# 128 tokens of a second expert ahead of the routing tail, one slot list, and out scatters that may overlap

## The chip, the cores and the metric

The kernel runs on one core of a Trainium2 chip. The core has five engines that work side by side: TensorE (PE) multiplies matrices, VectorE (DVE), ScalarE (ACT) and GpSimd (POOL) work on tiles, and SyncE (SP) issues most of the transfers. Each takes its instructions in the order in which they are queued. The metric is the device time of one execution in microseconds (us).

## The reference

An attention layer feeds a mixing layer with a two-matmul network (F = 2048), and that feeds a layer of eight experts. Only the last is touched by the change. Cut to what matters:

```python
B, S, D, E, F = (4, 576, 512, 8, 1024)
for b in range(B):
    prev_e = -1
    for s in range(S):
        fresh_e = argmax(logits[b, s])
        e = fresh_e if s == 0 or local_gate[b, s] < 0.5 else (prev_e if prev_e >= 0 else fresh_e)
        prev_e = e
        out[b, s] = p[e] * (relu(x[b, s] @ w1[e]) @ w2[e])
```

Every token goes to one expert. Which one depends on the tokens before it in its row of the batch, so an expert's last tokens are known only when the last rows of x are done.

## The kernel before

**Layout.** The 2304 tokens are 18 tiles of 128, taken in nine groups of two (the lists `GA` and `GB`). Matmuls take a number as a high and a low part (`split`: ScalarE casts the high part, VectorE subtracts for the low one), and `mm3` makes three matmuls of a product. `ffn` runs a two-matmul network in steps: for each of the eight 128-wide pieces f of the hidden layer 12 matmuls into `hps` (columns: the tokens), then ScalarE and VectorE make the hidden tile `h` (its ReLU and its low part) from it, and one step later 3 matmuls of 512 columns for each 128 tokens add into `acc`.

**The stages that the change touches.** While the mixing layer's second half runs over the groups 0 to 8, each finished group is routed: `finish_group` transposes its rows (`x2T`), `route` makes logits and one-hots, `assign` turns them into slot numbers, and GpSimd scatters an entry (row, token, gate) for each token into a list in HBM. An expert's slots are contiguous in it, in the order of its tokens. There are three lists (`slots0` to `slots2`), so that the last three scatters go to different ones; a reader loads all three and adds them.

After three of the four rows of the batch `first_expert` picks the expert with the most tokens so far, and `early` gathers its first 256 tokens (EARLY) and its weights: the early pass, an `ffn` over these, runs right behind group 8. Beside it, group 8 is routed and assigned, and `ranks` orders the experts: rank 0 is the early one, the others follow by size. Then one `ffn` runs for each rank, with room for CAPS[r] tokens (224 more of rank 0, 384 of rank 1, then 320, 320, 296, 272, 232, 216). What does not fit is done in a loop behind a branch, which these inputs do not take.

For each rank `expert_inputs` loads the slots, makes indices of them (`idn`), gathers the rows from `x2d` in HBM with an indirect transfer on GpSimd (`xg`), and transposes them (`tps`, then `xTe`). `expert_weights` loads 4 MB in four chunks of two 512 KB pieces into two raw tiles (`we`) and splits each piece in two. The split weights lie in two sets of four chunks (`wpA`, `wpB`), used in turn. `emit` scales the result by the gate (`yo`) and scatters it to `out`; each scatter waits for the one before, since both write `out`.

**What sets the order.** The code advances side work in generators (`beside`, `soon`, `pre_`) by some steps after each step of `ffn`. Each engine then has one fixed queue, in an order that the tool makes from this; `issue_after` keeps an instruction behind another.

Of the kernel before, what the change touches and what calls it, by code (L numbers as in the profile page):

```python
# [10 lines left out]
F32 = mybir.dt.float32  # L11
# [12 lines left out]
DM = H * D  # L24
# [14 lines left out]
EARLY = TM * P  # L39
CB = 256  # L40
# [32 lines left out]
CAPS = (224, 384, 320, 320, 296, 272, 232, 216)  # L73
# [20 lines left out]
LISTS = {GIDX[B - 1, 2]: 0, GIDX[B - 1, 3]: 1, GIDX[B - 2, 4]: 2}  # L94
NL = 3
# [16 lines left out]
def constants():  # L112
# [35 lines left out]
    c["rev"] = (float(E) - 1 - np.arange(E, dtype=np.float32))[None].copy()  # L148
    c["over"] = (P - 1 - np.array(CAPS, np.int32))[None].copy()
# [16 lines left out]
def build(ctx, tc, a, out):  # L166
# [5 lines left out]
    def split(hi, lo, src, eng=None):  # L172
        nc.scalar.copy(hi, src)  # L173
        return (eng or nc.vector).tensor_tensor(out=lo, in0=src, in1=hi.bitcast(F32), op=ALU.subtract)  # L174
# [33 lines left out]
    slots = [dram.tile([NSLOT, 4], F32, name=f"slots{i}") for i in range(NL)]  # L208
# [418 lines left out]
    def ffn(xT, n, chunks, ps_h, acc, hidden, sums, tail=0):  # L627
# [6 lines left out]
        for f in range(nf + 1):  # L634
# [16 lines left out]
            if f > 0:  # L651
# [3 lines left out]
                for t, c in enumerate(range(0, n, P)):  # L655
                    if g == 0:
                        acc.append(sums[t % len(sums)].tile([P, DM], F32, tag=("acc0", "acc1", "acc2", "g")[t], name="acc"))
# [5 lines left out]
                    mm3(acc[t][0:m], h[:, c:c + m], h[:, low + c:low + c + m], t2[:, 0, g % per], t2[:, 1, g % per], g == 0, g == nf - 1)  # L663
# [13 lines left out]
    rows_of, room = {}, []  # L677
# [125 lines left out]
    def setup():  # L803

        load = last["load"].ins
        with tc.issue_after(load):
            nc.sync.dma_start(out=ent, in_=a["ent"])
            for i in range(NL):
                nc.sync.dma_start(out=slots[i], in_=a["empty"][min(i, 1)])
# [309 lines left out]
    def assign(b, half=None):  # L1119
# [13 lines left out]
        for t in ts:  # L1133
# [12 lines left out]
            for j in range(2):  # L1146
# [15 lines left out]
    nc.sync.dma_start(out=over, in_=a["over"])  # L1162
    order = keep.tile([1, 2, E], F32, name="order")
# [3 lines left out]
    fid = keep.tile([1, 3, E], F32, name="fid")  # L1167
# [11 lines left out]
    def first_expert():  # L1179
# [6 lines left out]
        nc.vector.tensor_scalar(out=pre, in0=order[:, 0], scalar1=order[:, 1, 0:1], scalar2=float(EARLY), op0=ALU.is_equal, op1=ALU.mult)  # L1186
        xps = ps_g.tile([E, 1], F32, tag="g", name="xps")
        nc.tensor.transpose(xps, pre, ident[0:1, 0:1])
        nc.vector.tensor_tensor(out=carry, in0=carry, in1=xps, op=ALU.max)
        return nc.values_load(eid[0:1, 1, 0:1], engines=SP, min_val=0, max_val=E - 1)  # L1190

    def ranks():
# [6 lines left out]
        nc.vector.tensor_single_scalar(fid[:, 2], pre, 0.0, op=ALU.is_gt)  # L1199
        nc.vector.tensor_tensor(out=fid[:, 0], in0=order[:, 0], in1=fid[:, 2], op=ALU.mult)  # L1200
        nc.vector.scalar_tensor_tensor(out=order[:, 0], in0=fid[:, 2], scalar=-float(NONE), in1=order[:, 0], op0=ALU.mult, op1=ALU.add)
        nc.vector.max(out=fid[:, 1], in_=order[:, 0])
        nc.vector.tensor_reduce(out=order[:, 1, 0:1], in_=fid[:, 0], axis=AX.X, op=ALU.max)
        nc.vector.tensor_copy(order[:, 1, 1:E], fid[:, 1, 0:E - 1])
        experts_of()
        nc.vector.tensor_copy(fid[:, 2], eid[:, 1])
        nc.vector.tensor_single_scalar(fid[:, 1], fid[:, 2], float(CAP), op=ALU.mult)
        nc.vector.tensor_scalar_add(fid[:, 1, 0:1], fid[:, 1, 0:1], float(EARLY))
# [14 lines left out]
    def expert_weights(r, e):  # L1223
# [7 lines left out]
        if r < 0:  # L1231
# [23 lines left out]
            return  # L1255
        for c in range(F // CB):
# [265 lines left out]
```

## Time and profile before

| | us |
|---|---|
| median of 3 runs (lowest, highest) | 964.61 (963.09, 964.76) |
| the profiled execution | 962.21 |
| its span, from the first to the last instruction | 960.5 |
| TensorE busy | 900.8 |
| VectorE, ScalarE, GpSimd busy | 521.8, 379.6, 243.5 |
| mean granted TensorE clock | 0.978 |

TensorE is busy for 94% of the span, at the upper of its clock's two levels (2.4 GHz) in nearly every slice. Starts of instructions are given in us from the span's start. A matmul's shown duration overlaps the next one's: what a matmul costs in a row of equal ones is the distance of their starts.

### The profile page before, as it was taken

How to read it: one execution, taken by the hardware profiler on the slowest of the kernel's cores; microseconds unless marked ns; L12 is line 12 of the kernel's file. 1: busy time of each engine (PE TensorE's matmuls, PEld its weight loads, DVE VectorE, ACT ScalarE, POOL GpSimd, SP SyncE). 2: the span in 40 equal slices, each digit the busy share in tenths (PEclk: the TensorE clock that was granted, in tenths of full speed). 3: DMA queues.
4: the chain of work that ended last, by engine and by line, in shares of the span. 5: the costliest groups of instructions: out<-in, count | busy, mean ns of one | idle time of the engine just before them, and what ended most of it. 6: DMA issues, size and time to landing. Idle time of an engine off the chain costs nothing. (4 is left out here: it accounts for less than half of the span.)

```text
span 960.5 us, 16208 instructions
## 1 busy us (share of the span) xinstructions
PE 900.8 (94%) x5896; PEld 746.2 (78%) x5900; DVE 521.8 (54%) x1352; ACT 379.6 (40%) x993; POOL 243.5 (25%) x369
## 2 busy tenths in 40 slices
PE   8887899999999998999999999999979899999993
PEld 4645677776787897899988888887858799888782
DVE  5788666746746478411334435357655455556410
ACT  4674563653553245421121111114255354445310
POOL 2324531340222046210111312124123121122100
PEclk9999799999999999999999999999979999999997
DMA  9923161451403493263554442427077455455100
GB/s 313 358 79 122 58 213 43 149 167 39 131 26 100 148 347 114 66 154 67 111 110 110 102 108 49 107 77 242 23 234 263 136 178 190 164 186 174 65 20 20
DMA packets 109037, 128.82 MB, mean 134 GB/s; under 512 B 16222, under 2 KB 78046, under 8 KB 108884
## 3 DMA queue, kind: packets, MB, share of 16 engines
q1 hardware_dynamic: 83636, 103.62, 33.4%
q0 software_dynamic: 22720, 19.36, 9.3%
q10 hardware_dynamic: 2592, 4.72, 1.3%
q8 instruction: 48, 0.79, 0.3%
q14 instruction: 41, 0.34, 0.1%
HBM read 99.33 MB, written 30.87 MB: 136 GB/s over the span
## 5 line engine op out<-in xcount | busy, mean ns | idle before, releaser
L644 ACT ACTIVATE h<-hps 128x256 fp32r<-128x256 f32 x152 | 58.2, 383 | 276.3 <-PE hps L179 271.6
L647 DVE SCALAR_TENSOR_TENSOR h<-hps,h 128x256 fp32r<-128x256 f32 x152 | 63.7, 419 | 163.5 <-ACT h L644 163.3
L177 PE MATMUL acc<-t,h 128*128 128x512 f32 x304 | 126.7, 417 | 2.5 <-ACT h L644 1.4
L178 PE MATMUL acc<-t,h 128*128 128x512 f32 x304 | 121.3, 399 | 0.0
L179 PE MATMUL acc<-t,h 128*128 128x512 f32 x304 | 120.8, 398 | 0.4 <-DVE h L647 0.3
L174 DVE TENSOR_TENSOR t<-we,t 128x512 fp32r<-128x512 f32 x128 | 83.5, 686 | 44.9 <-ACT t L173 42.0
L179 PE MATMUL hps<-xT,t 128*128 128x256 f32 x288 | 83.6, 290 | 4.4 <-POOL t L174 4.4
L173 ACT CAST t<-we 128x512 fp32r<-128x512 f32 x128 | 73.5, 619 | 35.7 <-PE acc L661 17.4
L177 PE MATMUL hps<-xTe,t 128*128 128x320 f32 (+7 forms) x288 | 86.1, 300 | 1.2 <-ACT xTe L173 1.2
L177 PE MATMUL hps<-xT,t 128*128 128x256 f32 x288 | 85.0, 296 | 2.2 <-ACT t L173 1.7
L178 PE MATMUL hps<-xTe,t 128*128 128x320 f32 (+7 forms) x288 | 85.7, 297 | 0.0
L179 PE MATMUL hps<-xTe,t 128*128 128x320 f32 (+7 forms) x288 | 85.4, 296 | 0.0
L178 PE MATMUL hps<-xT,t 128*128 128x256 f32 x288 | 83.1, 289 | 0.6 <-DVE xT L174 0.6
L177 PE MATMUL hps<-xTb,t 128*128 128x256 f32 x288 | 83.2, 289 | 0.0
L179 PE MATMUL hps<-xTb,t 128*128 128x256 f32 x288 | 81.9, 284 | 0.0
L178 PE MATMUL hps<-xTb,t 128*128 128x256 f32 x288 | 81.7, 284 | 0.0
L412 ACT ACTIVATE t<-t,mx 128x128 f32<-128x128 f32 (+1 forms) x160 | 62.5, 393 | 38.5 <-DVE mx L405 34.4
L177 PEld LDWEIGHTS acc<-t,h 128*128 128x128 f32 x304 | 57.8, 190 | 15.9 <-issue 4.7
L179 PEld LDWEIGHTS acc<-t,h 128*128 128x128 f32 x304 | 57.2, 188 | 15.2 <-DVE h L647 1.8
L647 DVE SCALAR_TENSOR_TENSOR hE<-hps,hE 128x256 fp32r<-128x256 f32 (+4 forms) x96 | 30.8, 349 | 61.5 <-ACT hE L644 60.0
L178 PEld LDWEIGHTS acc<-t,h 128*128 128x128 f32 x304 | 57.9, 191 | 7.3 <-issue 0.2
L177 PEld LDWEIGHTS hps<-xT,t 128*128 128x128 f32 x288 | 56.0, 195 | 9.4 <-ACT t L173 2.7
(291 smaller groups left out, 2032.9 us busy)
## 6 DMA issues: line engine op xcount, KB each, us to landing
we<-in_w SPq DMA_DIRECT2D x64, 512.0 KB
rw<-in_w_ch SPq DMA_DIRECT2D x32, 512.0 KB
qkt<-in_qk SPq DMA_DIRECT2D x15, 642.0 KB
nd<-xT SPq DMA_DIRECT2D x18, 512.0 KB
xTb<-nd POOLq DMA_DIRECT2D x18, 512.0 KB, 7.9
vt<-in_v SPq DMA_DIRECT2D x16, 384.0 KB
pd<-y ACTq DMA_DIRECT2D x18, 256.0 KB
ub<-ud SPq DMA_DIRECT2D x18, 256.0 KB
```

The lines of the kernel that those rows point to most:

```text
L173: nc.scalar.copy(hi, src)
L174: return (eng or nc.vector).tensor_tensor(out=lo, in0=src, in1=hi.bitcast(F32), op=ALU.subtract)
L177: nc.tensor.matmul(o, lhsT=wh, rhs=xh, start=start, stop=False, **kw)
L178: nc.tensor.matmul(o, lhsT=wh, rhs=xl, start=False, stop=False, **kw)
L179: return nc.tensor.matmul(o, lhsT=wl, rhs=xh, start=False, stop=stop, **kw)
L412: nc.scalar.activation(t[0:m, j], t[0:m, j], AF.Exp, bias=mx[0:m, j:j + 1], scale=-1.0, accum_out=sums[0:m, j:j + 1])
L644: last["relu"] = nc.scalar.activation(h[:, 0:n], hps[:, 0:n], AF.Relu)
L647: last["rest"] = nc.vector.scalar_tensor_tensor(out=h[:, lo:lo + c1 - c0], in0=hps[:, c0:c1], scalar=0.0, in1=h[:, c0:c1].bitcast(F32), op ...
```

## The change

- `first_experts` picks two experts instead of one. The early pass of the larger one stays; the first 128 tokens of the second (NEXT) are gathered too and run as an `ffn` of their own behind it (the "next pass" below). Its weights are loaded as rank "-2" and kept: rank 1's main pass uses the same split weights for its other tokens, with room for 256 instead of 384.
- The entries go to one slot list. The last three scatters are declared free of one another, and the loads that read the list wait for all of them. Two of three slot loads and two adds fall away for each rank.
- Out scatters are declared free of the scatter just before.
- The rows of ranks 0 and 1 are both gathered during the next pass; rank 2's first weights are asked for behind rank 0's rows.

```diff
+NEXT = P
...
-CAPS = (224, 384, 320, 320, 296, 272, 232, 216)
+CAPS = (224, 256, 320, 320, 296, 272, 232, 216)
...
-LISTS = {GIDX[B - 1, 2]: 0, GIDX[B - 1, 3]: 1, GIDX[B - 2, 4]: 2}
-NL = 3
+TAIL = (GIDX[B - 1, 2], GIDX[B - 1, 3], GIDX[B - 2, 4])
...
-            nc.gpsimd.indirect_dma_start(out=slots[0 if first else LISTS.get(g, 0)], out_offset=IOA(ap=su[0:m], axis=0), in_=ent[0:m, g], in_offset=None,
+            w = nc.gpsimd.indirect_dma_start(out=slots, out_offset=IOA(ap=su[0:m], axis=0), in_=ent[0:m, g], in_offset=None,
                                          bounds_check=NSLOT - 1, oob_is_err=False)
+            if b == B - 1 and g in TAIL:
+                for x in placed:
+                    tc.declare_no_dep(w.ins, x, reason="each token has a slot of its own")
+                placed.append(w.ins)
             yield
...
-    def first_expert():
...
+    def first_experts():
...
+        nc.vector.tensor_scalar(out=fid[:, 0], in0=order[:, 0], scalar1=order[:, 1, 1:2], scalar2=float(NEXT), op0=ALU.is_equal, op1=ALU.mult)
+        nc.vector.tensor_tensor(out=pre, in0=pre, in1=fid[:, 0], op=ALU.add)
...
-        return nc.values_load(eid[0:1, 1, 0:1], engines=SP, min_val=0, max_val=E - 1)
+        return [nc.values_load(eid[0:1, 1, i:i + 1], engines=SP, min_val=0, max_val=E - 1) for i in range(2)]
...
+        def raw(c, behind_=None):
+            x = act.tile([P, 2, 4 * CB], F32, tag="xT", name="we")
+            x1, x2 = x[:, 0].rearrange("p (k f) -> p k f", k=4), x[:, 1].rearrange("p (k f) -> p k f", k=per)
+            w = nc.sync.dma_start(out=x1.unsqueeze(1), in_=w1[:, bass.ds(e, 1), :, c * CB:(c + 1) * CB])
+            if behind_ is not None:
+                tc.add_manual_dep(w.ins, behind_.name, mybir.DependencyInfo(mybir.DependencyClass.Sync, mybir.DependencyReason.DATA), reason="rows first")
+            nc.sync.dma_start(out=x2.unsqueeze(1), in_=w2[:, bass.ds(e, 1), c * per:(c + 1) * per, :])
+            return x1, x2
+
+        q = []
+        if r < 0:
+            q = [raw(0), raw(1)]
+            yield
         for c in range(F // CB):
             t1, t2 = chunksE[r][c]
-            x = act.tile([P, 2, 4 * CB], F32, tag="xT", name="we")
-            x1, x2 = x[:, 0].rearrange("p (k f) -> p k f", k=4), x[:, 1].rearrange("p (k f) -> p k f", k=per)
-            nc.sync.dma_start(out=x1.unsqueeze(1), in_=w1[:, bass.ds(e, 1), :, c * CB:(c + 1) * CB])
-            nc.sync.dma_start(out=x2.unsqueeze(1), in_=w2[:, bass.ds(e, 1), c * per:(c + 1) * per, :])
+            x1, x2 = q.pop(0) if r < 0 else raw(c, last["rows"].ins if r == 2 and c == 0 else None)
             for i in range(2):
                 m = slice(2 * i, 2 * i + 2)
                 split(t1[:, 0, m], t1[:, 1, m], x1[:, m])
                 yield
             for i in range(per):
                 split(t2[:, 0, i], t2[:, 1, i], x2[:, i])
+                if r < 0 and i == per - 1 and c + 2 < F // CB:
+                    q.append(raw(c + 2))
                 yield
...
+    wrote = []
+
+    def emit(acc, idx, m=P, both=False, alone=True):
         y = act.tile([P, DM], F32, tag="y", name="yo")
         if both:
...
+        w = nc.gpsimd.indirect_dma_start(out=out, out_offset=IOA(ap=idx[0:m, 1:2], axis=0), in_=y[0:m], in_offset=None,
+                                         bounds_check=NT - 1, oob_is_err=False)
+        if alone and wrote:
+            tc.declare_no_dep(w.ins, wrote[-1], reason="each token has one slot, so the rows are others")
+        wrote.append(w.ins)
+
+    def slot_load(s0, nt):
+        x = keep.tile([P, TE, 4], F32, tag="ids", name="ids", bufs=2)
+        w = nc.sync.dma_start(out=x[:, 0:nt], in_=slots[bass.ds(s0, nt * P)].rearrange("(t p) c -> p t c", p=P))
+        for y in placed:
+            tc.add_manual_dep(w.ins, y.name, mybir.DependencyInfo(mybir.DependencyClass.Sync, mybir.DependencyReason.DATA), reason="all slots written")
         return x
 
-    def slot_ids(x, nt, lists):
-
-        x0 = x[:, 0, 0:nt]
-        for i in range(1, lists):
-            nc.vector.tensor_tensor(out=x0, in0=x0, in1=x[:, i, 0:nt], op=ALU.add)
...
+        e, e2 = first_experts()
         pre_.add(expert_weights(-1, e))
+        more.append(e2)
         yield
         for _ in range(EL):
             yield
-        x = slot_load(e * CAP, TM, 1)
+        x = slot_load(e * CAP, TM)
+        y = slot_load(e2 * CAP, 1)
         for _ in range(2):
             yield
-        ids[-1] = slot_ids(x, TM, 1)
+        ids[-1] = slot_ids(x, TM)
+        ids[-2] = slot_ids(y, 1)
         xTs[-1] = lact.tile([P, 2, 4, TM * P], F32R, tag="xTe", name="xTe", bufs=1)
         gs = []
         for t in range(TM):
             g = act.tile([P, DM], F32, tag="h", name="xg", bufs=HB)
             nc.gpsimd.indirect_dma_start(out=g, out_offset=None, in_=x2d, in_offset=IOA(ap=ids[-1][:, t, 0:1], axis=0))
             gs.append(g)
+        g = lact.tile([P, DM], F32, tag="ub", name="xg")
+        nc.gpsimd.indirect_dma_start(out=g, out_offset=None, in_=x2d, in_offset=IOA(ap=ids[-2][:, 0, 0:1], axis=0))
+        more.append(g)
...
-        ids[r] = slot_entries(eb[r], nt, NL)
+        x = slot_load(eb[r], nt)
+        if r < 2:
+            yield
+        with behind() if r == 2 else nullcontext():
+            ids[r] = slot_ids(x, nt)
         xTs[r] = xp.tile([P, 2, 4, CAPM], F32R, tag="xT", name="xTe")
         rows = [min(P, CAPS[r] - t * P) for t in range(nt)]
         gs = []
+        if r == 1:
+            tags.append(tags.pop(0))
         for t in range(nt):
             gs.append(gather(ids[r][:, t], rows[t]))
             yield
         for t in range(nt):
-            transpose_split(xTs[r], t * P, gs[t], rows[t])
+            with nullcontext() if r > 1 else tc.issue_after(last["ffn" if r else "acc"].ins):
+                transpose_split(xTs[r], t * P, gs[t], rows[t])
             yield
 
     soon.drain()
     pre_.drain()
     acc = []
     xp = None
+    e2, g2 = more
+    xTs[-2] = wraw.tile([P, 2, 4, P], F32R, tag="r64", name="xTe", bufs=RB)
+    pre_.add(expert_weights(-2, e2))
+    pre_.step()
     for n, _ in enumerate(ffn(xTs.pop(-1), EARLY, chunksE[-1], ps_h, acc, hidden, (ps_a, ps_a))):
+        if n == 1:
+            with tc.issue_after(last["ffn"].ins):
+                transpose_split(xTs[-2], 0, g2)
+        with behind():
+            pre_.step(2 if n < 4 else n > 9)
         if xp is None:
             beside.step(2 if n < 4 else 1)
         if xp is None and not beside.q:
             c2.close()
             xp = ctx.enter_context(pool("xp", 2, reuse_waits="tile"))
-            pre_.add(expert_weights(1, er[1]))
-            pre_.step()
             beside.add(expert_inputs(0))
-            beside.step(TE)
-        elif xp is not None and n < 15:
-            pre_.step(2)
+            beside.step()
+            following = expert_inputs(1)
+            next(following)
     for t, x in enumerate(acc):
         emit(x, ids[-1][:, t])
+    acc = []
+    for n, _ in enumerate(ffn(xTs.pop(-2), NEXT, chunksE[-2], ps_h, acc, hidden, (ps_a2,), tags=("acc2",))):
+        with behind():
+            if n == 0:
+                beside.step(TM)
+            pre_.step()
+        if n == 14:
+            beside.step(TM)
     beside.drain()
-
-    chunksE[0] = chunksE[-1]
+    pre_.drain()
+    last["rows"] = last["hi"]
+    with tc.issue_after(last["hi"].ins):
+        emit(acc[0], ids[-2][:, 0])
+
+    chunksE[0], chunksE[1] = chunksE[-1], chunksE[-2]
...
-            beside.add(expert_inputs(r + 1))
+            beside.add(expert_inputs(r + 1) if r else following)
...
-            pre_.step(1 if r else 2)
+            pre_.step()
```

What this does to the queues is shown at three places. TensorE, at the end of the early pass: acc_7602 and acc_7652 are the second accumulator of that pass in the program before and of the change, xTe_7538 the 128 rows of the second expert, t1 its weights. Before:

```order
L179 MATMUL acc_7602<-t2_7135,h_7894 128x512
L177 MATMUL acc_7598<-t2_7135,h_7927 128x512
L178 MATMUL acc_7598<-t2_7135,h_7927 128x512
L177 MATMUL acc_7602<-t2_7135,h_7927 128x512
L616 MATMUL tps_7798<-ident_171,xg_7794 128x128 x4
L179 MATMUL acc_7598<-t2_7135,h_7927 128x512
L178 MATMUL acc_7602<-t2_7135,h_7927 128x512
L179 MATMUL acc_7602<-t2_7135,h_7927 128x512
L616 MATMUL tps_7954<-ident_171,xg_7796 128x96 x4
L177 MATMUL hps_7966<-xTe_7793,t1_7128 128x224
```

Now:

```order
L175 MATMUL acc_7652<-t2_7145,h_7927 128x512
L176 MATMUL acc_7652<-t2_7145,h_7927 128x512
L177 MATMUL acc_7652<-t2_7145,h_7927 128x512
L175 MATMUL hps_7958<-xTe_7538,t1_7539 128x128
L176 MATMUL hps_7958<-xTe_7538,t1_7539 128x128
...
L177 MATMUL acc_8002<-t2_7546,h_8095 128x512
L614 MATMUL tps_8120<-ident_169,xg_7978 128x128 x4
L614 MATMUL tps_8127<-ident_169,xg_7980 128x96 x4
L175 MATMUL acc_8002<-t2_7546,h_8114 128x512
```

The transposes of rank 0's gathered rows (`tps`) stood within the last six matmuls of the early pass; now the whole next pass but its last three matmuls stands between.

VectorE, behind group 8's result (`x`), where the early pass begins; `lg`, `rmx`, `oh` and `ex` are the routing's tiles, t_7539 to t_7542 the split weights of the second expert. Before:

```order
L1376 TENSOR_TENSOR x_7518<-acc,p__6922 128x512
L647 SCALAR_TENSOR_TENSOR h<-hps,h 128x256
L174 TENSOR_TENSOR x2T<-tps,x2T 128x4x128 x2
L647 SCALAR_TENSOR_TENSOR h<-hps,h 128x256
L1085 TENSOR_REDUCE lg<-pn 128x20
```

Now:

```order
L1400 TENSOR_TENSOR x_7535<-acc,p__6920 128x512
L645 SCALAR_TENSOR_TENSOR h<-hps,h 128x256
L172 TENSOR_TENSOR t_7539<-we,t_7539 128x512 x2
L172 TENSOR_TENSOR x2T<-tps,x2T 128x4x128 x2
L645 SCALAR_TENSOR_TENSOR h<-hps,h 128x256
L172 TENSOR_TENSOR xTe<-tps,xTe 128x512
L172 TENSOR_TENSOR t_7540<-we,t_7540 128x512 x2
L1082 TENSOR_REDUCE lg<-pn 128x20
L172 TENSOR_TENSOR t_7541<-we,t_7541 128x512
L1085 TENSOR_REDUCE rmx<-lg 128x2
```

Eight weight splits and the low part of the second expert's rows now stand among the routing's instructions (the last three splits follow a few rows further on); before, none did. ScalarE's queue has the casts that belong to them at the same places.

SyncE, from group 8's stores of x on; in_w are the experts' weights, eid and most are values that SyncE reads into registers. Before:

```order
L1377 DMA x2d<-x_7518 128x512
L1214 TENSOR_LOAD eid
...
L1260 DMA we<-in_w 128x4x256
...
L1261 DMA we<-in_w 128x2x512
...
L1293 DMA ids<-slots_115 128x2x4
...
L1293 DMA ids<-slots_116 128x2x4
```

Now:

```order
L1267 DMA we<-in_w 128x2x512
L1401 DMA x2d<-x_7532 128x512
...
L1264 DMA we<-in_w 128x4x256
...
L1219 TENSOR_LOAD eid
...
L1514 TENSOR_LOAD most
...
L1314 DMA ids<-slots 128x2x4
...
L1314 DMA ids<-slots 128x2x4
```

The second expert's eight weight loads are now ahead of the register loads, the first four of them ahead of group 8's stores of x. Nine register loads stand before the slot loads instead of four, and the slots of ranks 0 and 1 are loaded together.

## Rows read from the trace of the kernel before

**Rows 1.** The page's first part: busy time, share and instructions.

```profile
PE 900.8 (94%) x5896; PEld 746.2 (78%) x5900; DVE 521.8 (54%) x1352; ACT 379.6 (40%) x993; POOL 243.5 (25%) x369
```

**Rows 2.** Timeline of TensorE: start, duration, instruction, [idle before, releaser].

```profile
679.65 0.28 PE L177 MATMUL hps<-xTe,t 128*128 128x256 f32 x1
...
703.85 0.28 PE L179 MATMUL hps<-xTe,t 128*128 128x256 f32 x1
705.49 0.50 PE L177 MATMUL acc<-t,h 128*128 128x512 f32 x1 [1.36 <-ACT h L644]
...
711.73 0.66 PE L616 MATMUL tps<-ident,xg 128*128 128x128 f32 x4 [2.16 <-DMA xg<-x2d,idn]
...
714.61 0.90 PE L616 MATMUL tps<-ident,xg 96*128 96x96 f32 x4 [1.52 <-DMA xg<-x2d,idn]
716.66 0.77 PE L177 MATMUL hps<-xTe,t 128*128 128x224 f32 x2 [1.16 <-ACT xTe L173]
...
749.29 0.50 PE L179 MATMUL acc<-t,hE 128*128 128x512 f32 x1 [2.46 <-DVE hE L647]
...
779.63 0.30 PE L177 MATMUL hps<-xTe,t 128*128 128x320 f32 x1
```

**Rows 3.** Windows: length, busy us (instructions) of five engines, granted clock, DMA.

```profile
704.00:711.00 7.00, 3.93 (x11) 2.22 (x9) 5.13 (x13) 3.98 (x8) 2.93 (x2) 0.76 0.83 298
711.00:717.00 6.00, 2.60 (x12) 1.82 (x13) 3.54 (x6) 4.58 (x9) 1.01 (x1) 0.72 0.91 245
717.00:730.00 13.00, 13.00 (x81) 11.65 (x81) 9.03 (x24) 7.20 (x16) 7.23 (x7) 0.87 0.85 279
```

**Rows 4.** Timelines of the other engines, from the last slot scatter to the gather.

```profile
695.65 0.98 POOL L1155 DMA_INDIRECT slots<-ent,su  x1 [0.30 <-issue]
...
696.64 0.37 SPq L1260 DMA_DIRECT2D we<-in_w  x1
...
698.01 1.55 SPq L1293 DMA_DIRECT2D ids<-slots  x3
...
702.34 1.14 ACT L173 CAST t<-we 128x512 fp32r<-128x512 f32 x2 [3.41 <-DMA we<-in_w]
...
707.30 1.48 POOL L1275 DMA_INDIRECT xg<-x2d,idn  x1 [10.67 <-ACT t L173]
```

**Rows 5.** The page's DMA issues: count and median us to landing.

```profile
xg<-x2d,idn POOLq DMA_INDIRECT x23, 4.8
out<-yo,idn POOLq DMA_INDIRECT x23, 3.2
```

**Rows 6.** Timeline of VectorE in rank 1's pass.

```profile
746.01 0.17 DVE L1300 TENSOR_TENSOR ids<-ids 128x12 f32<-128x12 f32 x1 [4.38 <-DMA ids<-slots]
```

**Rows 7.** Timeline of TensorE: starts from which the distance of matmuls is read.

```profile
681.09 1.04 PE L616 MATMUL tps<-ident,x 128*128 128x128 f32 x8
...
769.22 0.33 PE L177 MATMUL hps<-xTe,t 128*128 128x384 f32 x1
...
771.32 0.39 PE L177 MATMUL acc<-t,hE 128*128 128x512 f32 x1
...
933.32 0.41 PE L177 MATMUL acc<-t,hE 128*128 128x512 f32 x1
...
934.72 0.26 PE L177 MATMUL hps<-xTe,t 128*128 128x216 f32 x1
...
936.05 0.41 PE L177 MATMUL acc<-t,hE 128*128 128x512 f32 x1
```

**Rows 8.** The weight splits by tile, 640 to 760 us: ns min/median/max.

```profile
L173 ACT CAST t<-we x54: 603/618/641, 651.8 to 758.9; 128x512 fp32r<-128x512 f32 x54
L174 DVE TENSOR_TENSOR t<-we,t x54: 654/684/693, 652.4 to 759.7; 128x512 fp32r<-128x512 f32 x54
```

**Rows 9.** Timelines of ScalarE and GpSimd at the end.

```profile
943.80 1.38 ACT L1286 ACTIVATE yo<-acc,idn 128x512 f32<-128x512 f32 x2 [1.75 <-PE acc L179]
944.77 1.00 POOL L1287 DMA_INDIRECT out<-yo,idn  x1 [16.91 <-ACT yo L1286]
949.03 1.00 POOL L1287 DMA_INDIRECT out<-yo,idn  x1 [3.26 <-issue]
```

**Rows 10.** Register loads of line 1214 on SyncE: ns min/median/max, first and last start.

```profile
L1214 SPq TENSOR_LOAD <-eid x8: 13/268/276, 693.0 to 726.8; - x8
```

More of the change, by code (lines that the diff above doesn't have):

```diff
@@ L172, in split @@
     def split(hi, lo, src, eng=None):
-        nc.scalar.copy(hi, src)
+        last["hi"] = nc.scalar.copy(hi, src)
         return (eng or nc.vector).tensor_tensor(out=lo, in0=src, in1=hi.bitcast(F32), op=ALU.subtract)
@@ L207, in build @@
     nd = [dram.tile([P, 2, 4, P], F32, name=f"nd{g}") for g in range(NG)]
-    slots = [dram.tile([NSLOT, 4], F32, name=f"slots{i}") for i in range(NL)]
+    slots = dram.tile([NSLOT, 4], F32, name="slots")
     ent = keep.tile([P, NG, 4], F32, name="ent")
@@ L625, in shift_of, with ffn @@
         return -(-m // 32) * 32
[L627 removed]
+    def ffn(xT, n, chunks, ps_h, acc, hidden, sums, tail=0, tags=("acc0", "acc1", "acc2", "g")):
         per = CB // P
@@ L662, in ffn @@
                         continue
-                    mm3(acc[t][0:m], h[:, c:c + m], h[:, low + c:low + c + m], t2[:, 0, g % per], t2[:, 1, g % per], g == 0, g == nf - 1)
+                    last["acc"] = mm3(acc[t][0:m], h[:, c:c + m], h[:, low + c:low + c + m], t2[:, 0, g % per], t2[:, 1, g % per], g == 0, g == nf - 1)
                 yield
@@ L807, in setup @@
             nc.sync.dma_start(out=ent, in_=a["ent"])
-            for i in range(NL):
-                nc.sync.dma_start(out=slots[i], in_=a["empty"][min(i, 1)])
+            nc.sync.dma_start(out=slots, in_=a["empty"])
             g0, g1 = GIDX[B - 1, 0], GIDX[B - 1, 3] + 1
@@ L1162, in build @@
     nc.sync.dma_start(out=over, in_=a["over"])
+    lead = keep.tile([1, E], F32, name="lead")
+    nc.sync.dma_start(out=lead, in_=a["lead"])
     order = keep.tile([1, 2, E], F32, name="order")
@@ L1166, in build @@
     pre = keep.tile([1, E], F32, name="pre")
-    fid = keep.tile([1, 3, E], F32, name="fid")
+    fid = keep.tile([1, 4, E], F32, name="fid")
     er, eb = [], []
@@ L1286, in emit, with slot_ids @@
             nc.scalar.activation(y[0:m], acc[0:m], AF.Copy, scale=idx[0:m, 2:3].bitcast(F32))
[L1287 to L1300 removed]
+        w = nc.gpsimd.indirect_dma_start(out=out, out_offset=IOA(ap=idx[0:m, 1:2], axis=0), in_=y[0:m], in_offset=None,
[8 more added lines that the diff above has]
+            tc.add_manual_dep(w.ins, y.name, mybir.DependencyInfo(mybir.DependencyClass.Sync, mybir.DependencyReason.DATA), reason="all slots written")
+        return x
+    def slot_ids(x, nt):
         n = keep.tile([P, TE, 3], U32, tag="idn", name="idn", bufs=E)
[L1302 to L1307 removed]
+        nc.vector.tensor_copy(n[:, 0:nt, 0:2], x[:, 0:nt, 0:2])
+        nc.vector.tensor_copy(n[:, 0:nt, 2:3].bitcast(F32), x[:, 0:nt, 2:3])
+        return n
     def early():
[L1311 removed]
+        e, e2 = first_experts()
         pre_.add(expert_weights(-1, e))
+        more.append(e2)
         yield
@@ L1335, in build @@
     beside, soon, pre_ = Beside(), Beside(), Beside()
+    more = []
     def fetch(j):
```

45 lines of the change are left out of this document (16 added, 29 removed).

## Prediction

> **What bounds the kernel now.** I read the page's busy times first: TensorE works for 94% of the span [rows 1], so time can only come from its waits, from a lower clock, or from its own work. The timeline of TensorE then shows where it waits in the stretch that the change rewrites, from the early pass's first matmul (679.65) to rank 2's first (779.63), which is 99.98 us. Five waits stand in it: 1.36, 2.16, 1.52 and 1.16 us between 705 and 717, and 2.46 us at 749, together 8.66 [rows 2]. The windows show a second cost: from 704 to 730 the granted clock is 0.76, 0.72 and 0.87 of the upper level of 2.4 GHz, that is, part of each window ran at 1.2 GHz [rows 3]. Counted as lost time this is 0.24 x 7 + 0.28 x 6 + 0.13 x 13 = 5.05 us. It fell while TensorE stood waiting, after a stretch without such waits.
>
> What it waited for is read backwards on the other engines. The transposes at 711.73 wait for gathered rows. The gather was issued at 707.30 and takes a median of 4.8 us to land [rows 4, 5]. It waited for the slot indices; the slots were asked for at 698.01, behind the last slot scatter of 695.65, but the adds that make indices of them stand on VectorE behind weight splits, and these follow ScalarE's casts, which began at 702.34, when the first weights of rank 1 had landed, 5.7 us after they were asked for at 696.64 [rows 4]. So routing, weights and gathers of the next rank all come due in the last matmuls of the early pass, with nothing for TensorE to do. The wait at 749 is of the same kind: VectorE stood 4.38 us in front of the slots of a later rank, with a hidden tile queued behind them [rows 6].
>
> **The change, part by part.** First what the stretch costs with no wait at full clock. The distance of matmuls, from starts: 12 matmuls of 256 columns take 681.09 - 679.65, or 0.120 each [rows 2, 7]; 12 of 384 columns 771.32 - 769.22, or 0.175; 12 of 216 columns 936.05 - 934.72, or 0.111; six of 512 columns 934.72 - 933.32, or 0.233 [rows 7].
>
> The early pass takes 24.20 us up to its last 256-column matmul at 703.85; with that one and the 12 of 512 columns left, 24.20 + 0.12 + 12 x 0.233 = 27.12. The row transposes are eight groups of four; the distance comes from the eight at 681.09, (1.04 - 0.28) / 7 = 0.109, where 0.28 is how long a lone matmul shows [rows 2, 7], so 32 x 0.109 = 3.49. The change keeps their number (1 + 2 + 2 + 3 groups against 2 + 3 + 3). Rank 0 (224 columns) takes 96 x 0.111 + 48 x 0.233 = 21.84, and rank 1 (384) 96 x 0.175 + 72 x 0.233 = 33.58.
>
> That is 86.03, so 13.95 us of the 99.98 are waits and clock; 8.66 + 5.05 accounts for all but 0.2.
>
> Added: the 384 columns of rank 1 become 128 and 256. The 256 cost 96 x 0.120 + 48 x 0.233 = 22.70. No row shows a matmul of 128 columns with new weights in these high and low parts. Between 384 and 256 columns the distance falls by 0.055; the same slope would give 0.065 at 128. But at 216 it is 0.111, not the 0.103 of that slope: something flat, the weight load that goes with each matmul, takes over. The transposes of 128 columns, each with new weights, stand at 0.109. I take 0.111 and keep 0.065 as the lower bound; 0.120 is the upper. The next pass then costs 96 x 0.111 + 24 x 0.233 = 16.25, and the two parts 38.95 against 33.58: 5.37 us more work.
>
> What it buys: between the early pass's end and rank 0's rows there are now 16 us of work. Is that enough? The routing now runs later, because eight splits of the second expert stand among it on VectorE and ScalarE. A split is 0.684 us on VectorE and 0.618 on ScalarE [rows 8]; eight and the low part of the new rows are 9 x 0.684 = 6.2 us, of which I find some 5 in front of the last slot scatter, the rest beside idle time. The scatter goes from 695.65 to about 700.7. If everything from it to the gather took as long as before, 707.30 - 695.65 = 11.65, the gather would start at 712.3, the second 1.3 later, and rank 0's rows would be there by 713.6 + 4.8 = 718.4. TensorE asks for them after 679.65 + 27.12 + 0.4 + 1.6 (new waits, below) + 16.25 - 0.7, at 724.3. Six us are to spare. So the waits at 711 to 717 go, the one at 705 too (weights are now asked for before the early pass), and with them the lower clock. So does the wait at 749: one slot load instead of three, queued on SyncE behind rank 2's first weights some 20 us before VectorE reads it. All 13.95 go.
>
> New waits. The routing has small matmuls in TensorE's queue. With VectorE late I get about 0.5 us each in front of the logits (`lps`) and their transpose (`pn`), and 0.3 each at the expert counts (`cps`) and the first slot transpose: 1.6. At rank 0's start its first matmuls need the low parts of rows transposed one step before: about 0.5. Together 2.1. The bounds: nothing, if the pass's slack swallows it; 6.2, if all of the nine VectorE instructions land on TensorE.
>
> The stretch: 13.95 - 5.37 - 2.1 = 6.5 us less.
>
> **The end.** ScalarE has both last tiles ready at 945.18; the first scatter starts at 944.77 and the second at 949.03, since it waits for the first to land (3.2 us by the median) [rows 5, 9]. The declaration names only the scatter just before, so a scatter still waits for the one two before it; for the last one that is rank 6's, over 20 us old. The last starts 0.30 us behind the first's end, as back-to-back issues on GpSimd do [rows 4, 9]: 944.77 + 1.00 + 0.30 = 946.07, 2.96 us less. In the middle of the program the out scatters are off TensorE's path, so I give them nothing.
>
> Queues passed. SyncE: the second expert's first four weight loads go ahead of group 8's stores of x, whose rows are gathered 30 us later, and nine register loads stand before the slot loads, not four; at 0.27 us and some 0.2 around it each, five more cost 2.2 us [rows 10], inside the six to spare. GpSimd: one gather more (1.3 us with its gap) ahead of two slot scatters 20 us before anybody reads them, and two out scatters ahead of rank 0's gathers, which start when the early pass's tiles are scaled, near 710. The fills of two lists and the adds fall away beside other work: nothing.
>
> **Sum.** 6.5 + 2.96 = 9.4 us. The profiled execution (962.21) is 2.4 below the median of the runs, which I take for its own scatter; by it the change gives 952.8, by the median 964.61 - 9.4 = 955.2.
>
> **Rivals.**
> *Cheaper 128 columns.* If the weight load hides at 128 columns, the slope's 0.065 holds: 96 x 0.046 = 4.4 us less, 950.8. Against it stand the equal rows at 216 columns and the transposes. Chance 0.12. The Trainium skill (TensorE: Matmul & The Clock Gate, Back-to-back issue gap) gives about 81 ns for a matmul of 128 columns in a stream of weight loads and matmuls, which as an estimate would give 2.9 us less, 952.3; no run here shows that size, and the rows of 216 columns and of the transposes lie above it.
> *The splits fill VectorE.* All 6.2 us come back as waits: 955.2 + 4.1 = 959.3. For it: the routing needs VectorE in many small steps. Against it: a hidden tile has some 2.8 us before its accumulation. Chance 0.15.
> *The end does not move*, because something else than the scatter's landing holds it: 958.2. Chance 0.07.
> *The second expert's weights come late (the other side).* Its second chunk reuses the raw tile that group 8's matmuls read until about 677. The cast of this chunk stands on ScalarE in front of the copy of the logits, at about 686. Landing as slowly as at 702.34, 5.7 us after the request, it is there at 683. Each us past 686 delays the routing's matmuls, and TensorE with them; past 695.5 the whole gain is gone and the kernel is slower, 966 and more if it lands at 697. Traffic is low before 680 and 3 us are to spare. Chance 0.09, of which 0.03 within the band below.
>
> **How the numbers follow.** The forecast has 0.57. A change under 0.2% (1.9 us) can't be told from none. Only the last rival reaches that band or crosses it: faster 0.91, same 0.03, slower 0.06. The range must leave out 0.2 at most: from 949.0 (the slope's 0.065 and no new wait: 955.2 - 4.4 - 2.1 = 948.7) to 961.5 (all of VectorE's time lost and most of the end's gain).
>
> **What will show it.** TensorE: no wait over 1 us between 700 and 730 and a clock of 1.00 there; 12 matmuls of 128 columns in 1.33 us (0.78 would be the rival); the next pass in about 16.3; rank 2's first matmul at about 773.1 instead of 779.63; the last two scatters 1.3 us apart. I am wrong if TensorE waits in the early pass for more than 3 us, if rank 0's rows still come after TensorE asks for them, or if the wait at 749 goes to another place in rank 1.

## The result, and the profile after

| | before | changed kernel |
|---|---|---|
| median (lowest, highest), us | 964.41 (963.09, 964.76) | 952.56 (947.77, 954.66) |
| ratio, 95% interval | 1 | 0.9889 (0.9858 to 0.992) |
| the profiled execution, its span | 962.21, 960.5 | 954.66, 952.8 |

The kernel is faster: 11.85 us by the medians, 7.7 by the spans of the two profiled executions. The profiled execution of before is faster than all four of its runs here, that of the changed kernel is the slowest of its four. A second measurement of the same kernel (below, a_again) gave 953.92 and a ratio of 0.992 (0.9889 to 0.9951). By its own pair of medians that is 8.8 us. Both intervals show a gain, and 9.4 us, the forecast, lies in both; as differences they reach from 7.7 to 13.7 and from 4.7 to 10.7 us.

The page's first line answers to [rows 1]: TensorE works 1.3 us longer, in a span that is 7.7 us shorter.

```profile
PE 902.1 (95%) x5992; PEld 749.9 (79%) x5996; DVE 521.9 (55%) x1348; ACT 380.9 (40%) x1001; POOL 246.0 (26%) x369
```

The timeline of TensorE answers to [rows 2]: the first matmuls of the early pass, the next pass, the ranks 0, 1 and 2, and every idle time over 0.3 us in between; at 711.04 and 712.33 a group of 12 matmuls of 128 columns begins and ends.

```profile
679.80 0.28 PE L175 MATMUL hps<-xTe,t 128*128 128x256 f32 x1
...
694.74 0.16 PE L1200 MATMUL cps<-ident,carry 8*1 8x8 f32 x1 [0.38 <-DVE carry L1124]
...
707.65 0.22 PE L175 MATMUL hps<-xTe,t 128*128 128x128 f32 x1
...
711.04 0.23 PE L175 MATMUL hps<-xTe,t 128*128 128x128 f32 x1
...
712.33 0.44 PE L175 MATMUL acc<-t,h 128*128 128x512 f32 x1
...
723.27 0.93 PE L614 MATMUL tps<-ident,xg 128*128 128x128 f32 x8
...
724.93 0.48 PE L175 MATMUL hps<-xTe,t 128*128 128x224 f32 x2
...
725.74 0.37 PE L176 MATMUL hps<-xTe,t 128*128 128x224 f32 x1 [0.33 <-DVE xTe L172]
...
748.34 0.28 PE L175 MATMUL hps<-xTe,t 128*128 128x256 f32 x1
...
758.47 0.63 PE L614 MATMUL tps<-ident,xg 128*128 128x128 f32 x4 [1.46 <-DMA xg<-x2d,idn]
...
773.99 0.30 PE L175 MATMUL hps<-xTe,t 128*128 128x320 f32 x1
...
937.80 0.40 PE L177 MATMUL acc<-t,hE 128*88 128x512 f32 x1
```

The stretch from the early pass's first matmul to rank 2's is 773.99 - 679.80 = 94.19 us, where it was 99.98 [rows 2]. The waits between 705 and 717 are gone, and rank 0's transposes at 723.27 wait for nothing. But at 758.47 stands a wait that was not there: TensorE wants rank 2's rows 1.46 us before they have landed.

The windows answer to [rows 3] (length, busy us of TensorE, its weight loads, VectorE, ScalarE and GpSimd with their counts, granted clock, transfers): the clock is at its upper level where it stood at 0.76, 0.72 and 0.87.

```profile
704.00:711.00 7.00, 7.00 (x48) 6.37 (x47) 3.98 (x11) 4.10 (x9) 2.26 (x3) 1.00 0.15 42
711.00:717.00 6.00, 6.00 (x46) 5.59 (x45) 1.65 (x5) 1.61 (x5) 2.99 (x3) 1.00 0.55 165
717.00:730.00 13.00, 12.67 (x91) 11.17 (x90) 3.10 (x9) 3.93 (x10) 1.96 (x2) 1.00 0.35 103
```

The timeline of GpSimd answers to [rows 4] and [rows 9]: the last slot scatter, the early pass's first out scatter and rank 0's gathers; rank 0's two out scatters with the gather of rank 2's rows behind them; and the last two out scatters.

```profile
700.62 1.24 POOL L1152 DMA_INDIRECT slots<-ent,su  x1 [0.85 <-DVE eid L1492]
...
708.13 0.98 POOL L1306 DMA_INDIRECT out<-yo,idn  x1 [6.27 <-ACT yo L1305]
...
710.71 1.00 POOL L1292 DMA_INDIRECT xg<-x2d,idn  x1 [0.31 <-DVE t L172]
712.01 1.31 POOL L1292 DMA_INDIRECT xg<-x2d,idn  x1 [0.30 <-issue]
...
748.82 1.01 POOL L1306 DMA_INDIRECT out<-yo,idn  x1 [21.88 <-ACT yo L1305]
750.13 1.17 POOL L1306 DMA_INDIRECT out<-yo,idn  x1 [0.30 <-issue]
753.11 1.44 POOL L1292 DMA_INDIRECT xg<-x2d,idn  x1 [1.81 <-issue]
...
938.50 0.99 POOL L1306 DMA_INDIRECT out<-yo,idn  x1 [19.50 <-ACT yo L1305]
939.80 1.01 POOL L1306 DMA_INDIRECT out<-yo,idn  x1 [0.30 <-issue]
```

The last slot scatter starts at 700.62 (700.7 was forecast) and rank 0's gather at 710.71 (712.3). The last two scatters are 1.30 us apart, where it was 4.26 [rows 9].

The timelines of VectorE and SyncE: the index conversions of rank 0 and, at 752, of ranks 2 and 3; the slot loads of ranks 2 and 3.

```profile
709.65 0.16 DVE L1322 CAST idn<-ids 128x4 uint32<-128x4 f32 x1
...
752.17 0.16 DVE L1322 CAST idn<-ids 128x6 uint32<-128x6 f32 x1
...
752.30 0.16 DVE L1322 CAST idn<-ids 128x6 uint32<-128x6 f32 x1
```

```profile
726.10 0.37 SPq L1314 DMA_DIRECT2D ids<-slots  x1
...
747.53 0.37 SPq L1314 DMA_DIRECT2D ids<-slots  x1
```

Where the time went is best read by stretches, from the starts in the timelines, since the early pass itself began anywhere from 676.2 to 680.2 in twelve profiled executions, with nearly the same work ahead of it. The stretches: from its first matmul to rank 2's first; from there to the last matmul; to the start of the last out scatter; and to the end of the span. Each row is one profiled execution.

| kernel | to rank 2 | to last matmul | to last scatter | to the end | sum |
|---|---|---|---|---|---|
| before | 99.98 | 164.44 | 4.96 | 11.47 | 280.85 |
| changed | 94.19 | 163.81 | 2.00 | 13.00 | 273.00 |
| a_again (the same) | 94.16 | 164.25 | 2.01 | 13.48 | 273.90 |
| b_scatter | 103.17 | 164.59 | 2.01 | 12.74 | 282.51 |
| b_list | 98.77 | 166.03 | 4.80 | 11.37 | 280.97 |
| b_parts | 98.54 | 164.55 | 2.01 | 11.97 | 277.07 |
| a_quarter | 86.50 | 164.56 | 2.00 | 12.31 | 265.37 |
| a_splits | 94.97 | 163.58 | 2.00 | 13.27 | 273.82 |
| a_mid | 94.37 | 163.93 | 2.02 | 13.76 | 274.08 |
| a_y4 | 94.18 | 162.25 | 2.01 | 13.00 | 271.44 |
| a_best | 94.30 | 162.27 | 2.01 | 12.27 | 270.85 |
| a_best2 | 92.52 | 162.25 | 2.01 | 12.57 | 269.35 |

### The profile page after: what moved, and what is told of

It is laid out like the page before. It is cut to its first block, busy times and chain, and to the rows that moved or that the text cites. A ratio compares the mean times of both kernels' runs of the same rounds, so it can differ in the third digit from the quotient of the medians.

```text
span 952.8 us, 16351 instructions
## 1 busy us (share of the span) xinstructions
PE 902.1 (95%) x5992; PEld 749.9 (79%) x5996; DVE 521.9 (55%) x1348; ACT 380.9 (40%) x1001; POOL 246.0 (26%) x369
## 4 chain that ended last, share of the span: by engine, by line
PE 70%; DVE 12%; issue 7%; DMA 5%; ACT 2%; POOL 2%; SPq 0%; POOLq 0%; DVEq 0%; ACTq 0%
PE hps L175 9%; PE hps L176 9%; PE hps L177 9%; PE acc L175 9%; PE acc L176 8%; PE acc L177 8%; PE o L438 3%; PE zps L588 2%; PE tps L614 2%; PE s L395 2%; DVE t L285 1%; PE acc L659 1%; PE pt L419 1%; DMA r<-ud 1%; PE xps L458 1%
## 5 line engine op out<-in xcount | busy, mean ns | idle before, releaser
L642 ACT ACTIVATE h<-hps 128x256 fp32r<-128x256 f32 (+1 forms) x160 | 60.5, 378 | 287.9 <-PE hps L177 284.6
L645 DVE SCALAR_TENSOR_TENSOR h<-hps,h 128x256 fp32r<-128x256 f32 (+1 forms) x160 | 66.1, 413 | 174.2 <-ACT h L642 173.7
L175 PE MATMUL acc<-t,h 128*128 128x512 f32 x312 | 130.1, 417 | 1.1 <-ACT t L171 1.0
L176 PE MATMUL acc<-t,h 128*128 128x512 f32 x312 | 124.5, 399 | 0.3 <-POOL t L172 0.3
L177 PE MATMUL acc<-t,h 128*128 128x512 f32 x312 | 124.5, 399 | 0.1
L176 PE MATMUL hps<-xTe,t 128*128 128x256 f32 (+7 forms) x320 | 91.8, 287 | 0.3 <-DVE xTe L172 0.3
L175 PE MATMUL hps<-xTe,t 128*128 128x256 f32 (+7 forms) x320 | 91.9, 288 | 0.0
L177 PE MATMUL hps<-xTe,t 128*128 128x256 f32 (+7 forms) x320 | 91.7, 287 | 0.0
L177 PEld LDWEIGHTS acc<-t,h 128*128 128x128 f32 x312 | 59.1, 190 | 14.6 <-issue 0.7
L175 PEld LDWEIGHTS acc<-t,h 128*128 128x128 f32 x312 | 59.3, 190 | 14.2 <-issue 4.7
L176 PEld LDWEIGHTS acc<-t,h 128*128 128x128 f32 x312 | 59.5, 191 | 7.8 <-POOL t L172 0.6
L175 PEld LDWEIGHTS hps<-xTe,t 128*128 128x128 f32 x320 | 60.6, 190 | 4.1 <-ACT xTe L171 0.4
L176 PEld LDWEIGHTS hps<-xTe,t 128*128 128x128 f32 x320 | 60.6, 190 | 3.1 <-DVE xTe L172 0.5
```

The lines of the kernel that those rows point to most:

```text
L175: nc.tensor.matmul(o, lhsT=wh, rhs=xh, start=start, stop=False, **kw)
L176: nc.tensor.matmul(o, lhsT=wh, rhs=xl, start=False, stop=False, **kw)
L177: return nc.tensor.matmul(o, lhsT=wl, rhs=xh, start=False, stop=stop, **kw)
L642: last["relu"] = nc.scalar.activation(h[:, 0:n], hps[:, 0:n], AF.Relu)
L645: last["rest"] = nc.vector.scalar_tensor_tensor(out=h[:, lo:lo + c1 - c0], in0=hps[:, c0:c1], scalar=0.0, in1=h[:, c0:c1].bitcast(F32), op ...
```

## The experiments

Each was measured beside the kernel before. The first two do one part of the change alone on that kernel, the third both. Gains given next to a ratio are worked out from the ratio, which differs a little from that of the two medians.

**b_scatter: the free out scatters alone.** (Not shown: the line that keeps the scatter as `w`.)

```diff
+        if alone and wrote:
+            tc.declare_no_dep(w.ins, wrote[-1], reason="each token has one slot, so the rows are others")
+        wrote.append(w.ins)
```

> The kernel before with the out scatters alone declared free of the scatter just before; nothing else is changed. My theory: the end loses the second scatter's wait for the first one's landing, 2.96 us, so about 961.4 against 964.4, with the last two scatters 1.3 us apart. Rival (the end does not move): 964.4. A second rival: freeing the scatters in the middle also moves gathers, which would show as a gain of more than 4 us.

Measured: 961.96 against 963.39, ratio 0.9983 (0.9965 to 1.0001), 1.6 us less with an interval from none to 3.4. The timeline of GpSimd shows the mechanism:

```profile
947.46 1.00 POOL L1289 DMA_INDIRECT out<-yo,idn  x1 [19.51 <-ACT yo L1288]
948.76 1.00 POOL L1289 DMA_INDIRECT out<-yo,idn  x1 [0.30 <-DVEq L1470]
```

The last scatter starts 2.95 us nearer to the last matmul (4.96 - 2.01), but the span ends 12.74 us behind it, not 11.47: some of the gain is given back. The profiled execution lost 3.2 us in the first stretch, with waits of 3.87 and 2.36 us there; its windows show a clock of 0.50 in 710 to 720 and 0.66 in 750 to 755. That is one execution; the median of twelve does not show such a loss.

**b_list: the one slot list alone.** `slots`, `TAIL`, `placed` and `slot_load` as in the change; the diff is that of the change at these lines.

> The kernel before with the one slot list alone (one load for each rank, no adds). My theory: the four waits between 705 and 717 stay, because TensorE still has nothing to do there; the wait of 2.46 us at 749 shrinks or goes, since the slot load that VectorE waits for takes 0.37 us of SyncE instead of 1.49 and two adds fall away. So 1.1 to 2.5 us less, 961.9 to 963.3. Rival (the one list is what shortens the junction): 5 us or more less, 959.4 or below.

Measured: 961.15 against 963.39, ratio 0.9979 (0.9959 to 0.9999), 2.0 us less, within what was expected of the list alone. The timeline of TensorE at the early pass's end (its first matmul is at 678.43 here):

```profile
708.31 1.11 PE L612 MATMUL tps<-ident,xg 128*128 128x128 f32 x4 [5.10 <-DMA xg<-x2d,idn]
...
709.65 0.63 PE L175 MATMUL acc<-t,h 128*128 128x512 f32 x1
710.07 0.63 PE L173 MATMUL acc<-t,h 128*128 128x512 f32 x1
...
713.70 0.49 PE L612 MATMUL tps<-ident,xg 96*128 96x96 f32 x4
715.60 0.48 PE L173 MATMUL hps<-xTe,t 128*128 128x224 f32 x2 [1.40 <-ACT xTe L169]
...
746.89 0.50 PE L175 MATMUL acc<-t,hE 128*128 128x512 f32 x1 [0.82 <-DVE hE L643]
```

The timeline of VectorE ahead of the last of these:

```profile
744.93 0.17 DVE L1299 CAST idn<-ids 128x6 uint32<-128x6 f32 x1 [4.06 <-DMA ids<-slots]
```

Counted from the early pass's first matmul the gather began 24.5 us later (702.90), 3.2 us sooner than before (27.65 [rows 2, 4]), and still rank 0's first matmul came 37.17 us behind the early pass's first, where it was 37.01 [rows 2]. The transposes now stood in TensorE's queue ahead of eleven matmuls of the early pass, not three; the engine waited 5.10 us for the rows, and then did most of those matmuls at the lower level, 0.42 us apart (710.07 - 709.65) where 0.233 is the distance at the upper one [rows 7]. Earlier rows bought nothing in this order; whether they would with the transposes queued behind those matmuls, no run shows. The wait at 749 fell from 2.46 to 0.82 us, with VectorE still standing 4.06 us in front of rank 3's slots.

The way from rank 2 to the last matmul is 1.6 us longer than before, and that is the clock: behind waits of 1.06 and 0.53 us in rank 6's pass it is 0.66 in 900 to 905, where the kernel before keeps 1.00 behind 1.06 and 0.58.

**b_parts: both, without the next pass.**

> The kernel before with the one slot list and the free out scatters together, without the next pass. My theory: the two parts are independent, 2.96 us at the end and 1.2 to 2.0 us in the middle, so about 4.5 us less, 0.9953 of the kernel before; what the changed kernel has beyond that, some 5 to 6 us, is the next pass. Rival (the parts bring the most of it together, because scatters, gathers and slot loads share GpSimd's queue): 8 us less or more, 0.9917. Other rival (they cancel): no change.

Measured: 958.93 against 963.83, ratio 0.9947 (0.9922 to 0.9971), 5.1 us less, where 4.5 were expected. The interval (2.8 to 7.5 us) leaves out both rivals and holds the sum of the parts, 3.6; the stretches of b_scatter and b_list, one execution each, do not show the gains. The next pass, with the order that comes with it, is worth the rest: 277.07 - 273.00, or 4.1 us by the stretches, a little less than I expected.

**a_quarter: the next pass cut to a quarter.** Three quarters of that pass's work are left out, so the 128 tokens get only a quarter of the sum. (Not shown in the diff: rank 0's transposes, which come at step 14 of that pass, come at step 2 here.)

```diff
-for n, _ in enumerate(ffn(xTs.pop(-2), NEXT, chunksE[-2], ...
+for n, _ in enumerate(ffn(xTs.pop(-2), NEXT, chunksE[-2][:1], ...
```

> The changed kernel with three quarters of the next pass's matmuls left out (only its first chunk of the hidden layer is computed, so those tokens' result is incomplete): 72 matmuls of 128 columns and 18 of 512 fewer, 12.2 us of TensorE's work. My theory: the next pass is cover; without it TensorE waits for rank 0's rows, which cannot be there before 716 or 717, so rank 0's first matmul comes near 719 instead of 724.9, and the clock falls again behind the wait. The time falls by 1 to 6 us, to 946.5 to 951.5 against 952.6. Rival (TensorE's work is all that counts there, rows and weights would have been early enough): 12.2 us less, 940.4.

Measured: 947.12, ratio 0.9819 (0.9788 to 0.9851), 5.4 us below the changed kernel's 952.56 by the medians, 7.7 by the first stretch, for 12.2 us of work. TensorE waits again:

```profile
713.96 1.11 PE L614 MATMUL tps<-ident,xg 128*128 128x128 f32 x4 [2.69 <-DMA xg<-x2d,idn]
...
716.71 0.77 PE L175 MATMUL hps<-xTe,t 128*128 128x224 f32 x2
```

The window behind it is at the lower level throughout (columns as above):

```profile
715.00:720.00 5.00, 4.91 (x21) 4.16 (x20) 1.25 (x2) 1.75 (x3) 1.33 (x2) 0.50 0.74 222
```

Rank 0's first matmul comes 37.08 us behind the early pass's, as in the kernel before (37.01), though a quarter of the next pass stands in between. So of the whole pass's 17.3 us only 8.1 lengthen the way to rank 0 (45.13 - 37.01): the pass is cover, as argued. My 719 for that matmul was 2.3 us late, because the first rows landed 3.4 us behind their gather at 710.54, not 4.8.

**a_splits: the second expert's splits behind the routing.**

```diff
-            pre_.step(2 if n < 4 else n > 9)
+            pre_.step(n > 9)
```

> The changed kernel with the second expert's eight early weight splits (and the loads of its later chunks) moved behind the routing. My theory: the splits delay the last slot scatter by some 5 us (700.6 back to about 696), but nobody on the path waits for it; TensorE's waits in the early pass are 0.4 us in the trace, so at most that is won: 951.5 to 953.5 against 952.6, the same within its scatter. Rival (the splits fill VectorE and cost TensorE 2 us or more): 950.5 or below.

Measured: 954.90, ratio 0.9916 (0.9887 to 0.9946); not told apart from the changed kernel. The last slot scatter came 16.2 us behind the early pass's start instead of 20.8, 4.6 earlier, and the stretch is 0.8 us longer. The time lies above the range expected, and the rival's gain of 2 us or more is not there: the early pass takes 27.54 us to the next pass's first matmul instead of 27.85, while the next pass, which now has these splits beside it, takes 18.37 instead of 17.28. The splits do delay the routing as forecast, and it costs TensorE 0.3 us at most.

**a_again, a_mid, a_y4, a_best: the two waits that are left.** The first is the changed kernel once more. In a_mid, rank 2's slot indices are made in the middle of rank 0's pass (`mark` is that pass's state at step 6):

```diff
-        with behind() if r == 2 else nullcontext():
+        with tc.issue_after(mark["rest"].ins) if r == 2 else nullcontext():
             ids[r] = slot_ids(x, nt)
```

In a_y4 the ranks' scaled results take the four tiles of `h`, which are free by then, instead of the two of `y`:

```diff
-        y = act.tile([P, DM], F32, tag="y", name="yo")
+        y = act.tile([P, DM], F32, tag=tag, name="yo", bufs=HB if tag == "h" else None)
```

> The changed kernel once more, beside the next three on the same chip. Expected: 0.989 of the kernel before, and again a wait near 1.5 us in rank 1's pass for rank 2's gathered rows, and 1.07 and 0.41 us in rank 5's pass. If the wait in rank 1's pass is absent here, it was an accident of one execution and not the queue on GpSimd.

> The changed kernel with rank 2's slot indices converted in the middle of rank 0's pass, so that its row gathers stand on GpSimd behind only one of rank 0's out scatters' predecessors and start near 736 instead of 753. My theory: the wait of 1.46 us at 758 comes from the late index conversion on VectorE and the two out scatters ahead of the gathers; it goes, rank 2's first matmul comes 1.5 us earlier, and the time is 1.5 us below the changed kernel's (0.9875 of before against 0.989). Rival (the wait moves: the conversion stands in front of hidden tiles, or rank 0's out scatters come behind the gathers and hold their tiles): no gain, with another wait of 1 us or more between 730 and 775.

> The changed kernel with four tiles for the scaled results of the ranks instead of two. My theory: the waits of 1.07 and 0.41 us in rank 5's pass come from the third result tile of a rank, which on ScalarE waits until the first out scatter has landed and stands there in front of a hidden tile; with a tile of its own they go: 1.5 us less than the changed kernel. Rival (ScalarE's or VectorE's order then brings another wait): no change.

> Both of the last two edits on the changed kernel. If the two waits are independent the gains add: 3.0 us less than the changed kernel, 0.986 of before. If one wait only covers for the other, less than 2 us.

Measured: 953.92, 952.86, 952.10 and 951.36 (before: 962.74); ratios 0.992 (0.9889 to 0.9951), 0.9888 (0.9858 to 0.9918), 0.9879 (0.985 to 0.9907) and 0.988 (0.9852 to 0.9909). The intervals overlap, so the stretches decide. In a_again the wait for rank 2's rows is there again, 1.44 us. The waits of 1.06 and 0.41 us are there again too; they stand at the start of rank 6's pass and come from rank 5's results. The timeline of ScalarE in the changed kernel shows how: the third result tile of rank 5 waits there for an out scatter, with a hidden tile behind it.

```profile
894.45 0.58 ACT L1301 COPY yo<-acc 16x512 f32<-16x512 f32 x1 [1.42 <-DMA out<-yo,idn]
895.05 0.62 ACT L642 ACTIVATE hE<-hps 128x232 fp32r<-128x232 f32 x2
```

In a_y4 the two waits are down to one of 0.40, and the way from rank 2 to the last matmul is 1.6 us shorter than in the changed kernel, nearly as expected. In a_mid the wait at 758 is gone, and the rival is right: another one stands in its place. TensorE, VectorE and SyncE of a_mid, one after another:

```profile
752.05 0.50 PE L177 MATMUL acc<-t,hE 128*128 128x512 f32 x1 [1.59 <-DVE hE L645]
```

```profile
750.23 0.17 DVE L1322 CAST idn<-ids 128x6 uint32<-128x6 f32 x1 [3.67 <-DMA ids<-slots]
```

```profile
746.14 0.37 SPq L1314 DMA_DIRECT2D ids<-slots  x1
```

VectorE stands 3.67 us in front of slots that were asked for only at 746.14, with a hidden tile behind it. They are rank 3's (rank 2's had been converted before its gather at 734.91). This is the wait of the kernel before [rows 6], in its old place. So the two edits do not add up in a_best: of the 3.0 us expected, 2.15 come by the stretches, 1.54 of them from the four tiles, 0.73 from the end and none from the way to rank 2, where a wait of 1.52 us stands at 751.

**a_best2: both edits, and rank 3's conversion kept behind the hidden tiles.** (The diff is against a_best.)

```diff
-        with tc.issue_after(mark["rest"].ins) if r == 2 else nullcontext():
+        with tc.issue_after(mark["rest"].ins) if r == 2 else behind() if r == 3 else nullcontext():
```

> The kernel with both edits, and rank 3's index conversion kept behind the hidden tiles as rank 2's was. My theory: the wait of 1.5 us at 751 that took the place of the one at 758 is VectorE standing in front of rank 3's slots; with that conversion later, none of the two is left and the way from the early pass's first matmul to rank 2's first falls from 94.3 to 92.8 us, the time 1.5 us below the version with both edits. Rival (the wait moves on, to rank 3's gathers in rank 2's pass or elsewhere): the way falls, but a wait of 1 us or more appears behind rank 2's first matmul, and the time stays.

Measured: 950.93 against 963.83, ratio 0.9874 (0.984 to 0.9908). The first stretch is 92.52 us, 1.67 below the changed kernel's, and TensorE has no idle time over 0.4 us between 696 and 893. Together with the four tiles this version is 3.65 us shorter than the changed kernel in the sum of the stretches. It is faster than the kernel before. Its median is the lowest of all versions that do the whole work, but its interval overlaps the changed kernel's; that it is faster than that one too rests on the stretches, of which the first differs by at most 0.21 us among the changed kernel, a_again, a_mid, a_y4 and a_best.

## Why the prediction was right

The forecast was 955.2 with a stretch 6.5 us shorter and an end 2.96 us earlier; the sum held, three of its terms did not. Part of the agreement is luck: the medians give 11.85 and 8.8 us, but the stretches, where the reasons lie, only 7.85 and 6.95.

- **The waits and the clock at 705 to 730**: right. All four waits went and the clock is 1.00. a_quarter shows why: with three quarters of the pass's work left out, a wait of 2.69 us and the lower clock return. Whether a shorter chain to the rows alone could have done it is open, since b_list also moved the transposes forward in the queue.
- **5.37 us more work**: right. Twelve matmuls of 128 columns take 712.33 - 711.04 = 1.29 us (1.33 forecast), and the next pass 724.93 - 707.65 = 17.28, of which eight transposes take 8 x 0.109 = 0.87; 16.41 remain against 16.25. The rival of cheaper columns falls. The Trainium skill's figure for such a stream, about 81 ns at 128 columns (TensorE: Matmul & The Clock Gate, Back-to-back issue gap), does not agree with this trace's 1.29 / 12 = 0.108 us; the measurement decides.
- **Rank 0's gather at 712.3**: it came 1.6 us earlier, and the forecast was near by luck. In a_splits the last slot scatter comes 4.6 us earlier and the gather only 0.3 (30.59 against 30.91 us behind the early pass's start), so it does not follow the scatter as the forecast had it. The indices are converted behind the next pass's first hidden tile, at 709.65 and without a wait, and two out scatters stand ahead of the gather on GpSimd. The time to spare made the mistake harmless.
- **"So does the wait at 749"**: this step failed, in the way that I had named. The slot load that I counted on, asked for 20 us before VectorE reads it, is rank 2's (726.10, read at 752.17). The slots that VectorE stood at in the kernel before were rank 3's, asked for only at 741.20. A shorter load makes that wait smaller, 0.82 us in b_list and 0.69 in b_parts, but does not remove it (1.59 us in a_mid, with one load too); that hangs on where the index conversion stands on VectorE. In the kernel before, rank 3's stood in front of a hidden tile. The change keeps rank 2's behind hidden tiles, and rank 3's follows it; then rank 2's comes so late (at 752.17, its gather at 753.11) that TensorE waits 1.46 us for the rows. a_mid and a_best2 tell the two apart.
- **2.1 us of new waits**: too much. The trace has 0.38 at `cps`, of which 0.26 was there before, and 0.33 at rank 0's start; the rest of the waits that I put into the early pass never came. a_splits, with the splits moved away, has an early pass only 0.3 us shorter, so VectorE's backlog cost TensorE no more than that there. The 1.4 us too many hide the 1.46 that I missed. That the stretch is 94.19 us long and not 93.5 lies in the work: without the waits shown it takes 92.0 us, not 86.03 + 5.37 = 91.4.
- **The end, 2.96 us**: right to the start of the last scatter (4.96 to 2.00), wrong behind it. I took the time from there to the span's end for unchanged; it is 11.4 and 11.5 us in the two kernels with waiting scatters, and 12.0 to 13.8, 12.8 on average, in the ten with free ones. So about 1.4 of the 2.96 is given back, and 1.6 is what b_scatter measured. Windows of 0.1 us show where: the core's last transfer ends 3.6 us behind the last scatter's start in both kernels with waiting scatters and 3.5 to 5.0, 4.1 on average, in the ten; and the span ends another 7.8 and 7.9 us later there, 8.5 to 8.8 here. Why either part takes longer, the trace does not show; I leave it open.
- **One list, "nothing"** beyond the wait at 749: not shown to be otherwise. The kernel before has a wait of 0.45 us at 845 for the adds of the lists, which is gone, and the way from rank 2 to the last matmul is 0.63 us shorter. But with the list alone the pass in which that wait stood (rank 4's) takes 30.00 us, as before (30.01), and only in the changed kernel 29.32; what shortened it stays open.
- **The rivals**: the splits among the routing do not fill VectorE's slack (0.3 us in a_splits), and the second expert's weights are not late (no wait for them in the stretch).

By the stretches the account is 5.79 + 0.63 + 2.96 - 1.53 = 7.85 us. The medians say 8.8 and 11.85; the start of the early pass alone differs by 4 us between executions, and what lies between may come from there; no run shows it.

## What to carry to other kernels

Where an engine waits at a junction, ask first whether other work of its own can stand there: 17.3 us of work put into the gap lengthened the way by 8.1, while a gather that came 3.2 us sooner bought nothing in the queue order that came with it. A small conversion in front of a hidden tile stalls TensorE when its data are late, and delays the gather that needs it when it is moved too far back; look for the place between. A gain at the end of a program counts only when the span's end moves with it.

## What the runs showed of the hardware that was not expected

- A wait can have a second price: behind 5.10 us of idle time, matmuls of 512 columns ran 0.42 us apart instead of 0.233 (b_list). But the 2.46 us at 749 left the clock of the kernel before at 1.00, and the same wait in b_scatter (2.62) was followed by a window at 0.66; and of two pairs of waits in rank 6's pass, the one of 1.06 and 0.58 us left it at 1.00 (before), the one of 1.06 and 0.53 was followed by 0.66 (b_list). In the second pair it is the longer waits that left the clock up, so their length alone does not decide it; what does, no run shows.
- With two indirect scatters in flight the program's span ended later behind the start of the last one than with two in sequence: 12.0 to 13.8 us in ten kernels against 11.4 and 11.5 in two.
